# RWKV-5 attention and soft-MoE slots on one core: diagonal product from SBUF copies, one masked state product, a gated first weight, halved first output tiles

## The chip, the cores and the metric

The kernel runs on one core of a Trainium2 chip. A core has TensorE (PE, with its weight loads shown as PEld), VectorE (DVE), ScalarE (ACT), GpSimd (POOL) and SyncE (SP), which run their own instruction streams and meet through semaphores, and 16 DMA engines that serve the queues of SP and POOL. The metric is the device time of one execution in microseconds (us). The kernel before takes 125.46 us (median of three runs, 125.38 to 126.85).

## What is computed

The first stage is a linear attention with a decaying state, for batch 4, 8 heads, sequence 768, head size 48. The second is a soft mixture of experts over all 3072 rows of 384 values, with 8 experts, 4 slots each and a hidden size of 1024.

```python
for t in range(S):
    kt, vt, rt = (k[:, :, t], v[:, :, t], r[:, :, t])
    cur = np.einsum('bhd,bhe->bhde', u[None] * kt, vt)
    y[:, :, t] = np.einsum('bhd,bhde->bhe', rt, state + cur)
    state = w[None, :, :, None] * state + np.einsum('bhd,bhe->bhde', kt, vt)
...
x = y.transpose(0, 2, 1, 3).reshape(B * S, H * D)
logits = x @ phi
# d: softmax of logits over the rows, c: softmax over the slots
slot_input = d.T @ x
for e in range(E):
    h = np.maximum(slot_input[e] @ w1[e], 0.0)
    slot_out[e] = h @ w2[e]
out = c @ slot_out
```

The term with u is the diagonal: for each row, the sum over d of r, u and k at that row, times v.

## The kernel before

**Units.** Two heads side by side (96 columns, or 2 x 64 partitions after a transpose) make a unit m; there are 4 batches x 4 pairs of heads = 16 units. Each unit is cut into G = 2 halves of T = 384 rows, and each half into L = 3 chunks of 128 rows. The loop variable i counts halves: i = 2m for the first, 2m + 1 for the second, 32 in all, and it starts at -5 so that loads and transposes of later units run ahead.

**Steps of a half or a unit**, with the engine that does them:

- `scale` (L228, POOL; DVE for unit 0): k and r from `raw` times a table of powers of w (`W`), into `kr` in bf16. Three `kr` tiles rotate.
- `t_pe` (L235, PE): six transposes each of k (into PSUM bank T0, in even iterations) and r (into T1, in odd ones); `t_evac` (L241, ACT) copies them to `kT` and `rT` in SBUF.
- `b_pe`, `b_evac` (L247 PE, L252 DVE): k back to rows, `kn`.
- `prod_f` (L257, DVE): r times k, element by element, with r read from T1 and k from `kT`, both in a strided order. `prod` goes to PE (L329) to be summed against u.
- `a_pe`, `mask_f` (L299 PE, L304 DVE): the 128 x 128 blocks of r and k products for the chunks, masked into `AT`.
- `m_pe` (L314, L325, L329, PE): state products and diagonal sums in the PSUM bank Mb. `z_evac` (L339, L343, L345, DVE) takes them out: `Z0` (the state carried to the second half, times w to the power T, only for g = 0), `Z` (the states inside the half), both masked with `bmask` to the two heads' blocks, and `dv` (v times the diagonal sums).
- `y_pe`, `y_evac` (L355, L366, L368 PE, L375 ACT): the half's output.
- `v_cast`, `v_pe`, `v_evac` (L270, L284, L290): v to bf16, reordered through PE.

Every engine's stream is in the order in which the program is written; the helper `O` keeps it. In iteration i DVE gets `mask_f(i+1)`, in even iterations `prod_f`, then `z_evac(i+1)`, and in odd ones the copy to `kn`. PE gets `a_pe(i+1)`, `y_pe(i)`, `v_pe(i+2)`, `m_pe(i+1)`, routing steps (from i = 8 on, for the batch before: transposes of x, logits with phi, dispatch sums) and the transposes.

**Loads.** SP's queue holds the inputs: k, r and v of batches 0 and 1 in quarters, phi, then batches 2 and 3 as one transfer each of k, r and v. Three `raw` tiles hold the batches; batch 3 goes into that of batch 0. POOL's queue holds the weights, cast to bf16 on the way: eight of w1, eight of w2 (the last in three pieces), issued between the `kr` products as the table `W_AT` says. w2 goes into `raw` 1 and 2 when their batches are done.

**End.** The slot inputs `uns`, the expert matmuls (L594, then transposes L617, then L627), the division by the softmax sums over rows (`so`), row sums of the other softmax (L608, with their reciprocals L610), and 24 output tiles (L646 PE; L648 DVE and L650 ACT scale them), stored by SP and POOL in groups of 1, 1, 2, 4, 4, 4, 4, 4 tiles (L652).

Of the kernel before, what the change touches and what calls it, by code (L numbers as in the profile page):

```python
# [9 lines left out]
def kernel(  # L10
# [106 lines left out]

    def load_batch(b, step):
        for h0 in range(0, H, step):
            load_kr(0, k, b, h0, h0 + step)  # L120
            load_kr(1, r, b, h0, h0 + step)
            load_v(b, h0, h0 + step)

    load_batch(0, 2)
    load_batch(1, 2)
    O(sp.dma_start(out=phi_f[:], in_=moe_phi.rearrange("(mo p) s -> p mo s", p=128)))
    load_batch(2, H)
# [16 lines left out]
    O(pool.iota(s_i, pattern=[[-1, J]], base=T - 1, channel_multiplier=-J))  # L144
    ident_f = cst.tile([128, 128], f32, name="ident_f")
    O(pool.memset(ident_f[:], 0.0))
    O(pool.affine_select(out=ident_f[:], in_=ident_f[:], compare_op=ALU.not_equal, fill=1.0, base=0,
                         pattern=[[-1, 128]], channel_multiplier=1))
# [19 lines left out]
    ident = cst.tile([128, 128], bf, name="ident")  # L168
    O(dve.tensor_copy(ident[:], ident_f[:]))

# [25 lines left out]
    ex(1, 1)  # L196
    bmask = cst.tile([128, P2], f32, name="bmask")
    ones = cst.tile([128, 128], bf, name="ones")
    ucol = cst.tile([128, nQ, 2], bf, name="ucol")
    Le_t = [cst.tile([128, L, 128], bf, name=f"Le{j}") for j in range(2)]  # L200
    uns = cst.tile([128, nM, 2, EG, 32], bf, name="uns")
    O(pool.memset(bmask[:], 0.0))
    O(pool.memset(bmask[0:64, 0:D], 1.0))
    O(pool.memset(bmask[64:128, D:P2], 1.0))
    O(pool.memset(ones[:], 1.0))
    O(pool.memset(ucol[:], 0.0))
    for t in Le_t:
        O(pool.memset(t[:], 0.0))
    O(pool.memset(uns[:], 0.0))
    O(pe.transpose(Mb[:, 0:8], wu[:], ident_f[0:8, 0:8]))  # L210
# [43 lines left out]
    def prod_f(m):  # L254
        pr = wk.tile([128, S], bf, name="prod", bufs=2)
        st["prod", m] = pr
        O(dve.tensor_mul(pr[:].rearrange("p (s j) -> p s j", j=J),  # L257
                         T1[:, 0:S].rearrange("p (j s) -> p s j", j=J),
                         st["kT", m][:].rearrange("p (s j) -> p s j", j=J)))

# [71 lines left out]
    def z_evac(i):  # L332
        m, b, q, g, n = at(i)
        dv = wk.tile([128, L * 2, D], bf, name="dv", bufs=2)
        st["dv", i] = dv
        if g == 0:
            Z0 = wk.tile([128, P2], bf, name="Z0", bufs=2)
            st["Z0", m] = Z0
            O(dve.scalar_tensor_tensor(out=Z0[:], in0=Mb[:, 2 * P2:3 * P2], scalar=wT[:, q:q + 1],  # L339
                                       in1=bmask[:], op0=ALU.mult, op1=ALU.mult))  # L340
        Z = wk.tile([128, 2, P2], bf, name="Z", bufs=2)
        st["Z", i] = Z
        O(dve.tensor_mul(Z[:], Mb[:, 0:2 * P2].rearrange("p (c e) -> p c e", c=2),  # L343
                         bmask[:, None, :].to_broadcast([128, 2, P2])))
        O(dve.tensor_mul(dv[:], st["v", i][:].rearrange("p c e d -> p (c e) d"),  # L345
                         Mb[:, 288:288 + 2 * L, None].to_broadcast([128, L * 2, D])))

    def y_pe(i):
# [9 lines left out]
        for c in range(L):  # L358
            if c == 0:
                if g == 0:  # L360
                    continue
                z = st["Z0", m][:]
# [29 lines left out]
    def xt_ev(n, c, xt=None, eng=None):  # L392
        xT = wk.tile([128, Dm], bf, name="xT", bufs=4)
        st["xT", n, c] = xT
# [70 lines left out]

    W_AT = {13: 1, 14: 1, 15: 1, 16: 1, 18: 1, 19: 1, 21: 1, 22: 1, 23: 1, 25: 1, 26: 5}
    T_AT = {-4: [(dve, 0, 2), (dve, 1, 2), (act, 0, 2)], -3: [(act, 1, 2), (dve, 0, 3)],
            -2: [(act, 0, 3)], -1: [(dve, 1, 3), (act, 1, 3)]}
    nw = 0
    n0, n1 = nG - 2, nG - 1  # L470
    Wf = [t[:].rearrange("p q j d -> p (q j d)") for t in W]
    xs = Wf[0].bitcast(bf)[:, 2 * F:2 * F + 2 * L * Dm].rearrange("p (n m c t) -> p n m c t", n=2, m=nM, c=L)

# [141 lines left out]
    for g in range(2):  # L615
# [22 lines left out]
    obuf = ([raw[0][:, 16 * Dm:17 * Dm], raw[0][:, 17 * Dm:18 * Dm], Wf[0][:, 0:2 * Dm], Wf[1][:, 0:4 * Dm]]  # L638
            + [raw[0][:, x * 4 * Dm:(x + 1) * 4 * Dm] for x in range(4)])
    i = 0  # L640
    for gi, sz in enumerate(sizes):
        o_s = obuf[gi][:, 0:sz * Dm].rearrange("p (n m) -> p n m", m=Dm)
        i0 = i
        for j in range(sz):
            op = ob[i % 6][:, 0:Dm]
            O(pe.matmul(op, LexpT[:, i:Nn:nN], so[:], start=True, stop=True))  # L646
            if i % 2 == 0:
                O(dve.tensor_scalar_mul(o_s[:, j, :], op, rsr[:, i:i + 1]))  # L648
# [36 lines left out]
```

## Time and profile before

| what | value |
|---|---|
| median of three runs | 125.46 us |
| profiled execution, its own time | 124.32 us |
| its span in the trace | 122.5 us |
| mean granted TensorE clock | 0.967 |
| busy: PE, DVE, ACT, POOL | 100.0, 97.3, 84.2, 62.5 us |
| DVE products, prod L257 | 16 x 947 ns |
| DVE products, AT L304 | 32 x 950 ns |
| DVE, Z0 L339; Z L343; dv L345 | 16 x 317; 32 x 347; 32 x 444 ns |
| POOL, kr L228 | 30 x 1459 ns |
| HBM read, written | 39.38 MB, 4.72 MB |

An engine's busy time is the sum of its instructions. Two instructions that follow each other directly overlap by some tens of ns in these records, so the time that one takes in a row of its kind is its distance from start to start. The rows of forty digits cut the span into slices of 3.06 us. The chain of waits goes back from the last instruction: at each step to what released it, or to the instruction before it on its engine. A name in square brackets behind a row of the timeline is what ended the idle time before it.

### The profile page before, as it was taken

How to read it: one execution, taken by the hardware profiler on the slowest of the kernel's cores; microseconds unless marked ns; L12 is line 12 of the kernel's file. 1: busy time of each engine (PE TensorE's matmuls, PEld its weight loads, DVE VectorE, ACT ScalarE, POOL GpSimd, SP SyncE). 2: the span in 40 equal slices, each digit the busy share in tenths (PEclk: the TensorE clock that was granted, in tenths of full speed). 3: DMA queues.
4: the chain of work that ended last, by engine and by line, in shares of the span. 5: the costliest groups of instructions: out<-in, count | busy, mean ns of one | idle time of the engine just before them, and what ended most of it. 6: DMA issues, size and time to landing. Idle time of an engine off the chain costs nothing.

```text
span 122.5 us, 4329 instructions
## 1 busy us (share of the span) xinstructions
PE 100.0 (82%) x1784; PEld 80.5 (66%) x1785; DVE 97.3 (79%) x200; ACT 84.2 (69%) x176; POOL 62.5 (51%) x75
## 2 busy tenths in 40 slices
PE   5698988898898998989899898999979799994000
PEld 1356866686687877979778797777878549962000
DVE  1998899999999999899999999999978235598000
ACT  4479768777868798886889887788858253397000
POOL 5899999995756778494687758110000000011100
PEclk9999999999999999999999999999999999999655
DMA  2999999999999999999999999999999992069992
GB/s 66 290 372 374 372 372 366 347 388 362 328 384 372 324 217 215 212 219 212 217 218 211 220 209 215 216 217 218 215 214 215 210 193 49 5 235 395 401 415 94
DMA packets 21093, 31.79 MB, mean 259 GB/s; under 512 B 1361, under 2 KB 18258, under 8 KB 21074
## 3 DMA queue, kind: packets, MB, share of 16 engines
q0 software_dynamic: 3088, 14.95, 55.1%
q1 hardware_dynamic: 17986, 16.57, 40.1%
q8 instruction: 14, 0.23, 0.7%
q14 instruction: 5, 0.04, 0.1%
HBM read 39.38 MB, written 4.72 MB: 360 GB/s over the span
## 4 chain that ended last, share of the span: by engine, by line
DVE 38%; PE 31%; issue 11%; POOL 7%; ACT 4%; DVEq 1%; POOLq 1%; ACTq 0%
DVE prod L257 11%; DVE AT L304 8%; DVE dv L345 6%; DVE Z L343 5%; PE Vb L284 5%; DVE raw L648 3%; PE Mb L325 3%; PE Yb L368 3%; PE T L235 3%; PE T L425 2%; PE T L247 2%; POOL kr L228 2%; PE Ab L299 1%; DVE kn L252 1%; ACT W L484 1%
## 5 line engine op out<-in xcount | busy, mean ns | idle before, releaser
L228 POOL TENSOR_TENSOR kr<-raw,W 128x576 bf16<-128x576 f32 x30 | 43.2, 1459 | 14.6 <-PE T L235 11.1
L304 DVE TENSOR_TENSOR AT<-Ab,mask_ut 128x768 bf16<-128x768 f32 x32 | 30.4, 950 | 1.0 <-PE Ab L299 1.0
L284 PEld LDWEIGHTS <-Q 128*128 128x128 bf16 x288 | 16.2, 100 | 3.6 <-issue 2.9
L284 PE MATMUL Vb<-v_bf,Q 128*128 128x96 bf16 x288 | 18.2, 211 | 0.0
L235 PE MATMUL T<-ident,kr 128*128 128x128 bf16 x192 | 17.0, 230 | 0.2 <-POOL kr L228 0.2
L241 ACT COPY rT<-T 128x768 bf16<-128x768 bf16 x16 | 12.8, 798 | 6.0 <-PE T L235 2.7
L241 ACT COPY kT<-T 128x768 bf16<-128x768 bf16 x16 | 12.8, 799 | 5.1 <-PE T L235 4.8
L257 DVE TENSOR_TENSOR prod<-T,kT 128x768 bf16<-128x768 bf16 x16 | 15.1, 947 | 0.0
L375 ACT CAST x<-Yb 128x288 bf16<-128x288 f32 x32 | 13.1, 410 | 2.8 <-PE Yb L368 2.8
L652 POOL DMA_DIRECT2D out_dram<-W x1 | 0.5, 541 | 27.2 <-ACT raw L650 27.2
L345 DVE TENSOR_TENSOR dv<-vn,Mb 128x288 bf16<-128x288 bf16 x32 | 14.2, 444 | 0.0
L366 PE MATMUL Yb<-Z,rT 128*128 128x96 bf16 x80 | 10.5, 204 | 3.8 <-DVE Z L343 3.8
L290 ACT CAST vn<-Vb 128x288 bf16<-128x288 f32 x32 | 13.1, 409 | 0.5
L235 PEld LDWEIGHTS <-kr 128*128 128x128 bf16 x192 | 12.6, 102 | 1.1 <-DVE kr L228 0.5
L299 PE MATMUL Ab<-rT,kT 64*128 64x128 bf16 x192 | 11.1, 222 | 0.6 <-DVE AT L304 0.5
L325 PE MATMUL Mb<-vn,kn 128*128 128x96 bf16 (+2 forms) x80 | 11.5, 243 | 0.0
L343 DVE TENSOR_TENSOR Z<-Mb,bmask 128x192 bf16<-128x192 f32 x32 | 11.1, 347 | 0.0
L355 PE MATMUL Yb<-vn,AT 128*128 128x48 bf16 x192 | 10.3, 185 | 0.0
L368 PE MATMUL Yb<-dv,ident 128*128 128x288 bf16 x32 | 9.1, 284 | 1.4
L270 ACT CAST v_bf<-raw 128x576 bf16<-128x576 f32 x15 | 10.1, 676 | 0.0
L252 DVE COPY kn<-T 128x768 bf16<-128x768 bf16 x16 | 8.9, 555 | 1.4 <-PE T L247 0.7
L355 PEld LDWEIGHTS <-AT 128*128 128x128 bf16 x192 | 6.9, 96 | 3.2
(141 smaller groups left out, 209.4 us busy)
## 6 DMA issues: line engine op xcount, KB each, us to landing
w_all<-in_moe_w_dram POOLq DMA_DIRECT2D x8, 768.0 KB, 10.3
raw<-in_moe_w_dram POOLq DMA_DIRECT2D x7, 768.0 KB, 14.7
raw<-in_k_dram SPq DMA_DIRECT2D x8, 288.0 KB, 6.1
raw<-in_r_dram SPq DMA_DIRECT2D x8, 288.0 KB, 6.0
raw<-in_v_dram SPq DMA_DIRECT2D x8, 288.0 KB, 6.1
raw<-in_k_dram SPq DMA_DIRECT2D x2, 1152.0 KB, 10.9
raw<-in_r_dram SPq DMA_DIRECT2D x2, 1152.0 KB, 9.9
raw<-in_v_dram SPq DMA_DIRECT2D x2, 1152.0 KB, 13.1
```

What stands on the lines that cost most here:

```text
L228: O(eng.tensor_mul(kr[:, j].rearrange("p j (h s) -> p j h s", s=64)[:, :, :, 0:D], src, W[j][:, q].rearrange("p j (h d) -> p j h d", h=2)))
L235: O(pe.transpose(bank[:, x * C:(x + 1) * C], kr[:, j, x, :], ident[:]))
L241: O(act.copy(t[:].rearrange("p (s j) -> p s j", j=J), bank[:, 0:S].rearrange("p (j s) -> p s j", j=J)))
L257: O(dve.tensor_mul(pr[:].rearrange("p (s j) -> p s j", j=J), T1[:, 0:S].rearrange("p (j s) -> p s j", j=J), st["kT", m][:].rearrange("p (s ...
L284: O(pe.matmul(Vb[:, c * P2:(c + 1) * P2], Q3[:, o:o + C], vb[:, :, g, j, :], start=(j == 0), stop=(j == JV - 1)))
L290: O(act.copy(vn[:].rearrange("p c e d -> p (c e d)"), Vb[:, 0:L * P2]))
L304: O(dve.tensor_mul(AT[:], Ab[:, :, 0:T].rearrange("p e (c t) -> p e c t", c=L), mask_ut[:, None, None, :].to_broadcast([128, 2, L, C])))
L325: O(pe.matmul(o, kn[:, g * L + c, :], vc, start=first, stop=True, skip_group_check=True))
L343: O(dve.tensor_mul(Z[:], Mb[:, 0:2 * P2].rearrange("p (c e) -> p c e", c=2), bmask[:, None, :].to_broadcast([128, 2, P2])))
L345: O(dve.tensor_mul(dv[:], st["v", i][:].rearrange("p c e d -> p (c e) d"), Mb[:, 288:288 + 2 * L, None].to_broadcast([128, L * 2, D])))
L355: O(pe.matmul(Yb[:, o:o + D], AT[:, e, c, :], vn[:, c, e, :], start=first, stop=False, skip_group_check=True))
L375: O(act.copy(st["x", n][:, :, q * P2:(q + 1) * P2], Yb[:, 0:L * P2].rearrange("p (c e) -> p c e", c=L)))
```

## The change

- `prod_f` reads r from `rT` in SBUF instead of the PSUM bank T1, both operands in plain order, and stands behind `z_evac(i+1)` instead of ahead of `y_pe(i)`.
- `bmask` becomes a table `zt` per pair of heads, with three blocks of 96 columns, the third multiplied by w to the power T. One product gives Z and Z0 (288 columns for g = 0, 192 for g = 1). POOL fills the table at the start.
- The last batch's v is loaded as three quarters and one quarter. A one-column copy on POOL (`guard`) of the first piece stands ahead of the first weight, and `W_AT` moves the first weights from i = 13, 14 to 15 (two at once).
- `phi_f` and `ident_f` lie in `LexpT`, `uns` in a part of the table `W[1]` (zeroed at i = 28 instead of the start), and `xT` has two buffers instead of four.
- The first two output tiles are each computed and scaled in two halves of 192 columns, one on DVE, one on ACT. The reciprocals of the row sums are issued apart from the sums and later.

```diff
@@ loads
-    def load_batch(b, step):
+    def load_batch(b, step, cut=0):
         for h0 in range(0, H, step):
             load_kr(0, k, b, h0, h0 + step)
             load_kr(1, r, b, h0, h0 + step)
-            load_v(b, h0, h0 + step)
+            load_v(b, h0, h0 + step - cut)
+            if cut:
+                load_v(b, h0 + step - cut, h0 + step)
...
@@ start
-    bmask = cst.tile([128, P2], f32, name="bmask")
+    zt = cst.tile([128, nQ, 3, P2], f32, name="zt")
...
-    O(pool.memset(bmask[:], 0.0))
-    O(pool.memset(bmask[0:64, 0:D], 1.0))
-    O(pool.memset(bmask[64:128, D:P2], 1.0))
+    O(pool.memset(zt[:], 0.0))
+    O(pool.memset(zt[0:64, :, :, 0:D], 1.0))
+    O(pool.memset(zt[64:128, :, :, D:P2], 1.0))
...
-    O(pool.memset(uns[:], 0.0))
...
+    O(pool.tensor_mul(zt[:, :, 2, :], zt[:, :, 2, :], wT[:, :, None].to_broadcast([128, nQ, P2])))
...
@@ prod_f
-        O(dve.tensor_mul(pr[:].rearrange("p (s j) -> p s j", j=J),
-                         T1[:, 0:S].rearrange("p (j s) -> p s j", j=J),
-                         st["kT", m][:].rearrange("p (s j) -> p s j", j=J)))
+        O(dve.tensor_mul(pr[:], st["rT", m][:], st["kT", m][:]))
...
@@ z_evac
+        x = 3 if g == 0 else 2
+        Z = wk.tile([128, x, P2], bf, name=f"Z{g}", bufs=2)
+        st["Z", i] = Z
         if g == 0:
-            Z0 = wk.tile([128, P2], bf, name="Z0", bufs=2)
-            st["Z0", m] = Z0
-            O(dve.scalar_tensor_tensor(out=Z0[:], in0=Mb[:, 2 * P2:3 * P2], scalar=wT[:, q:q + 1],
-                                       in1=bmask[:], op0=ALU.mult, op1=ALU.mult))
-        Z = wk.tile([128, 2, P2], bf, name="Z", bufs=2)
-        st["Z", i] = Z
-        O(dve.tensor_mul(Z[:], Mb[:, 0:2 * P2].rearrange("p (c e) -> p c e", c=2),
-                         bmask[:, None, :].to_broadcast([128, 2, P2])))
+            st["Z0", m] = Z[:, 2, :]
+        O(dve.tensor_mul(Z[:], Mb[:, 0:x * P2].rearrange("p (c e) -> p c e", c=x), zt[:, q, 0:x, :]))
...
@@ loop
-    W_AT = {13: 1, 14: 1, 15: 1, 16: 1, 18: 1, 19: 1, 21: 1, 22: 1, 23: 1, 25: 1, 26: 5}
+    W_AT = {15: 2, 16: 1, 18: 1, 19: 1, 21: 1, 22: 1, 23: 1, 24: 1, 25: 1, 26: 5}
...
-        if odd == 0 and 0 <= mu + 1 < nU:
-            prod_f(mu + 1)
...
             z_evac(i + 1)
+        if odd == 0 and 0 <= mu + 1 < nU:
+            prod_f(mu + 1)
...
         if i == 3:
-            load_batch(3, H)
+            load_batch(B - 1, H, 2)
...
+        if i == min(W_AT):
+            O(pool.tensor_copy(guard[:], raw_of(2, B - 1)[:, 0:1]))
+        if i == 28:
+            O(pool.memset(uns, 0.0))
...
@@ output
+    def emit(i, bank, dst, x0, x1, eng):
+        op = ob[bank % 6][:, 0:x1 - x0]
+        O(pe.matmul(op, LexpT[:, i:Nn:nN], so[:, x0:x1], start=True, stop=True))
+        if eng is dve:
+            O(dve.tensor_scalar_mul(dst[:, x0:x1], op, rsr[:, i:i + 1]))
+        else:
+            O(act.activation(out=dst[:, x0:x1], in_=op, func=AF.Copy, scale=rsr[:, i:i + 1]))
...
+            if i < 2:
+                emit(i, 2 * i, o_s[:, j, :], 0, HD, dve)
+                emit(i, 2 * i + 1, o_s[:, j, :], HD, Dm, act)
             else:
+                emit(i, i + 2, o_s[:, j, :], 0, Dm, (dve, act)[i % 2])
             i += 1
+            if i == 2:
+                row_recip(8, 16)
+            if i == 6:
+                row_sums(16, nN)
+            if i == 8:
+                row_recip(16, nN)
```

More of the change, by code (lines that the diff above doesn't have):

```diff
@@ L98 @@
     warm = LexpT[:, 2048:2560]
+    late = LexpT[:, 2560:3072].bitcast(f32)
+    ident_f = late[:, 0:128]
+    phi_f = late[:, 128:128 + nM * ES].rearrange("p (m s) -> p m s", m=nM)
     wu = cst.tile([8, 128], f32, name="wu")
     wu3 = wu[:].rearrange("q (e s) -> q e s", s=64)
-    phi_f = cst.tile([128, nM, ES], f32, name="phi_f")
     O(act.preload_act_table_set("natural_log_exp_and_others"))
@@ L121, in load_batch @@
             load_kr(1, r, b, h0, h0 + step)
-            load_v(b, h0, h0 + step)
+            load_v(b, h0, h0 + step - cut)
+            if cut:
+                load_v(b, h0 + step - cut, h0 + step)
     load_batch(0, 2)
     load_batch(1, 2)
-    O(sp.dma_start(out=phi_f[:], in_=moe_phi.rearrange("(mo p) s -> p mo s", p=128)))
+    O(sp.dma_start(out=phi_f, in_=moe_phi.rearrange("(mo p) s -> p mo s", p=128)))
     load_batch(2, H)
@@ L144 @@
     O(pool.iota(s_i, pattern=[[-1, J]], base=T - 1, channel_multiplier=-J))
-    ident_f = cst.tile([128, 128], f32, name="ident_f")
-    O(pool.memset(ident_f[:], 0.0))
-    O(pool.affine_select(out=ident_f[:], in_=ident_f[:], compare_op=ALU.not_equal, fill=1.0, base=0,
+    O(pool.memset(ident_f, 0.0))
+    O(pool.affine_select(out=ident_f, in_=ident_f, compare_op=ALU.not_equal, fill=1.0, base=0,
                          pattern=[[-1, 128]], channel_multiplier=1))
@@ L168 @@
     ident = cst.tile([128, 128], bf, name="ident")
-    O(dve.tensor_copy(ident[:], ident_f[:]))
+    O(dve.tensor_copy(ident[:], ident_f))
     keep_warm(4)
@@ L200 @@
     Le_t = [cst.tile([128, L, 128], bf, name=f"Le{j}") for j in range(2)]
-    uns = cst.tile([128, nM, 2, EG, 32], bf, name="uns")
-    O(pool.memset(bmask[:], 0.0))
-    O(pool.memset(bmask[0:64, 0:D], 1.0))
-    O(pool.memset(bmask[64:128, D:P2], 1.0))
+    O(pool.memset(zt[:], 0.0))
+    O(pool.memset(zt[0:64, :, :, 0:D], 1.0))
+    O(pool.memset(zt[64:128, :, :, D:P2], 1.0))
     O(pool.memset(ones[:], 1.0))
@@ L217 @@
     O(act.activation(out=wT[:], in_=wT[:], func=AF.Exp, scale=float(T)))
+    O(pool.tensor_mul(zt[:, :, 2, :], zt[:, :, 2, :], wT[:, :, None].to_broadcast([128, nQ, P2])))
     phi_s = cst.tile([128, nM, ES], bf, name="phi_s")
     acc = cst.tile([128, NA], f32, name="acc")
+    guard = cst.tile([128, 1], f32, name="guard")
     st = {}
@@ L361, in y_pe @@
                     continue
-                z = st["Z0", m][:]
+                z = st["Z0", m]
             else:
@@ L392, in xt_ev @@
     def xt_ev(n, c, xt=None, eng=None):
-        xT = wk.tile([128, Dm], bf, name="xT", bufs=4)
+        xT = wk.tile([128, Dm], bf, name="xT", bufs=2)
         st["xT", n, c] = xT
@@ L471 @@
     Wf = [t[:].rearrange("p q j d -> p (q j d)") for t in W]
+    uns = Wf[1].bitcast(bf)[:, 2 * F:2 * F + nM * ES * 8].rearrange("p (m g j x) -> p m g j x", m=nM, g=2, j=EG)
     xs = Wf[0].bitcast(bf)[:, 2 * F:2 * F + 2 * L * Dm].rearrange("p (n m c t) -> p n m c t", n=2, m=nM, c=L)
@@ L609, in row_sums, with row_recip @@
                         start=(i == a), stop=(i == z - 1), skip_group_check=True))
+    def row_recip(a, z):
         O(dve.reciprocal(rsr[:, a:z], Mb[:, a:z]))
@@ L621 @@
             row_sums(0, 8)
+    row_recip(0, 8)
     SO = [Xb[:, 0:HD], Yb[:, 0:HD]]
@@ L644 @@
         for j in range(sz):
[L645 to L648, printed above, removed]
+            if i < 2:
+                emit(i, 2 * i, o_s[:, j, :], 0, HD, dve)
+                emit(i, 2 * i + 1, o_s[:, j, :], HD, Dm, act)
             else:
-                O(act.activation(out=o_s[:, j, :], in_=op, func=AF.Copy, scale=rsr[:, i:i + 1]))
+                emit(i, i + 2, o_s[:, j, :], 0, Dm, (dve, act)[i % 2])
             i += 1
+            if i == 2:
[4 more added lines that the diff above has]
+                row_recip(16, nN)
         O((sp, pool)[gi % 2 if gi > 1 else 0].dma_start(out=out_v[:, i0:i, :], in_=o_s))
-        if gi == 2:
-            row_sums(16, nN)
 _INS = ['r', 'k', 'v', 'w', 'u', 'moe_phi', 'moe_w1', 'moe_w2']
```

## The prediction

> **What bounds the kernel now.** I read the page's busy shares and its 40 slices first, to find which resource never rests.
>
> ```profile
> PE 100.0 (82%) x1784; PEld 80.5 (66%) x1785; DVE 97.3 (79%) x200; ACT 84.2 (69%) x176; POOL 62.5 (51%) x75
> ...
> DVE  1998899999999999899999999999978235598000
> ...
> DMA  2999999999999999999999999999999992069992
> GB/s 66 290 372 374 372 372 366 347 388 362 328 384 372 324 217 215 212 219 212 217 218 211 220 209 215 216 217 218 215 214 215 210 193 49 5 235 395 401 415 94
> ```
>
> DVE is at 9 tenths through the attention loop (to about 92 us), and so is the DMA row, from 3 us to 101 us. Two things therefore run side by side: DVE's loop, and one unbroken stream of transfers, first the inputs (about 370 GB/s), then the MoE weights (about 215 GB/s). Whichever is last decides when the expert matmuls can end. The table of stretches shows where the stream changes over, and the DMA answer for the last weight piece (issued at 81.49) when it lands.
>
> ```profile
> core 0: us, PE busy (x) PEld busy (x) DVE busy (x) ACT busy (x) POOL busy (x), PEclk, DMA share, GB/s
> 2.00:40.00 38.00, 32.91 (x473) 25.00 (x472) 34.97 (x70) 28.17 (x55) 32.74 (x38) 1.00 1.07 356
> 40.00:42.00 2.00, 2.00 (x44) 1.77 (x42) 1.94 (x5) 1.54 (x5) 1.50 (x3) 1.00 1.21 349
> 42.00:44.00 2.00, 1.73 (x34) 1.28 (x32) 2.00 (x5) 1.58 (x3) 1.64 (x2) 1.00 1.11 242
> 44.00:100.00 56.00, 51.14 (x1035) 43.22 (x1038) 48.57 (x101) 43.63 (x100) 24.21 (x28) 1.00 1.04 214
> 100.00:104.00 4.00, 4.00 (x116) 3.25 (x112) 2.10 (x5) 1.77 (x3) 0.00 (x0) 1.00 0.48 86
> ```
>
> ```profile
> L134 POOL DMA_DIRECT2D raw<-in_moe_w_dram x1: 527/527/527, 81.5 to 81.5; - x1
> ...
> DMA to landing us min/median/max: 22.3/22.3/22.3
> ```
>
> The DMA share is 1.0 or more in every stretch up to 100, so no time is free in the stream. The last w2 piece (steps y = 6 and 7 of expert 7) lands at 81.49 + 22.3 = 103.8. Its first reader, step y = 6 of the second half of L627, is due at 105.0 (in the chain the L627 matmuls run from 102.61 to 105.36, 0.17 for a step y of each half). The slack is only 1.2 us: **a faster loop alone gains at most that; a later stream costs all beyond it.**
>
> **The loop.** One pair of iterations costs DVE, start to start in the timeline from 31.56: AT 0.87, prod 0.86, Z 0.26, dv 0.36, AT 0.86, idle 0.28, Z0 0.23, Z 0.27, dv 0.36, kn 0.47: 4.8 us. PE waits about 0.7 to 0.9 in such a pair (for Z, dv, and Ab), and about 0.55 where routing is interleaved.
>
> *prod from SBUF.* 16 times. The trace has no bf16 product with both operands in SBUF. Upper end: today's row, 0.95 (the f32 products of L182, 744 ns for 576 elements, give the same at 768). Lower end: the 768-element bf16 copy to kn, 0.56. I take the lower one, as the price most favourable to the change, and keep 0.95 for the top of the range: a gain of 0.40 a pair, or none. For comparison only: the Trainium skill, "VectorE: DVE Perf Modes", section "The perf-mode tier table", gives a bf16 tensor_tensor in SBUF two elements a cycle, and its (N/2 + 150) cycles would make 0.56 of it, an estimate from that page; no run here shows it, and by it the sum stays as it is.
>
> *One Z product.* Z0 (0.23) goes, Z grows by 96 columns (0.10 at the 0.96 elements/ns of AT): gain 0.13. With dv no longer behind prod, PE's next steps start 0.86 earlier, and the idle 0.28 of DVE goes too. Together up to 0.8 a pair, and PE (about 4.0 us of work) would be next.
>
> *What comes back.* POOL's kr scaling reads two SBUF tiles. The loop products of DVE today each read PSUM, so they never meet it; the L182 products at the start do:
>
> ```profile
> 9.34 1.21 DVE L182 TENSOR_TENSOR W<-LexpT,sr 128x576 f32<-128x576 f32 x1
> 11.02 0.56 DVE L252 COPY kn<-T 128x768 bf16<-128x768 bf16 x1 [0.47 <-PE T L247]
> 11.50 0.94 DVE L182 TENSOR_TENSOR W<-LexpT,sk 128x576 f32<-128x576 f32 x1
> ```
>
> ```profile
> 8.87 1.06 POOL L268 CAST v_bf<-raw 128x576 bf16<-128x576 f32 x1
> 9.90 1.92 POOL L228 TENSOR_TENSOR kr<-raw,W 128x576 bf16<-128x576 f32 x1
> ```
>
> Alone they take 0.74. The first ends at 10.55, 0.62 after POOL's cast (9.93); the second at 12.44, 0.62 after POOL's kr (11.82). And that kr took 1.92 instead of 1.41, ending 1.27 after the DVE product. Each waited for the other to finish. So a prod that meets a kr waits for up to 1.36 (kr's start-to-start time). Where it falls in steady state:
>
> ```profile
> 62.85 0.95 DVE L257 TENSOR_TENSOR prod<-T,kT 128x768 bf16<-128x768 bf16 x1
> 62.89 0.50 PE L235 MATMUL T<-ident,kr 128*128 128x128 bf16 x6
> 63.55 1.40 POOL L228 TENSOR_TENSOR kr<-raw,W 128x576 bf16<-128x576 f32 x1 [0.38 <-PE T L235]
> ```
>
> In the new order Z and dv (0.62) stand in prod's place and prod's turn is at 63.47, 0.08 before kr: a coin toss. Without routing PE's transposes end sooner: prod's turn is 32.43 + 0.62 = 33.05, kr runs 32.64 to 34.04, so prod waits 1.0. Earlier still POOL runs thirteen kr back to back (9.90 to 29.25): mean wait 0.68. Per pair: -0.8 + 0.68 to 1.0, that is -0.1 to +0.2. Behind a waiting prod stand DVE's next AT and PE's diagonal matmuls (L329), and behind these the transposes that release POOL. Over the five pairs up to the first weight I count 0.1. The rule that speaks against the change is in the skill's "SBUF — State Buffer", section "Who interferes with whom": a DVE instruction with two SBUF inputs and a GpSimd one that reads SBUF exclude each other for the whole instruction, whoever starts first. Read merely as a slowing (0.20 and 0.47 in the two rows) the pairs would gain 0.4 each and the first weight come 2 us sooner; by the rule the sum stays.
>
> *Start.* POOL gets longer before its first kr, and that kr is on the chain:
>
> ```profile
> 9.90 1.93 POOL kr L228
> 11.83 0.05 issue
> 11.88 0.82 PE T L235 x6
> ```
>
> Its memsets run at (0.745 - 0.209)/640 = 0.84 ns an element. The table zt of 1152 columns costs 1.07, its two half fills of 576 cost 0.58 each, its product with wT (384 elements, between ucol's 0.60 for 4 and kr's 1.41 for 576) 1.14: 3.4. Gone: bmask 0.17 + 0.13 + 0.13, uns 0.74: 1.2. Less 0.1 for overlapping starts, +2.1 on the loop, bounds +1.2 (zt product at 0.60, half fills hidden) to +2.5. The uns memset returns at i = 28 behind the w2 issues, which queue far ahead of the stream: nothing. Smaller xT rings, ident_f and phi_f moved: nothing, each buffer's reader is one iteration on.
>
> **The first weight.** Before, it is issued at 39.48, behind POOL's seventeenth kr, while the inputs still flow. After, the guard copy and the first two weights stand behind the nineteenth kr, and wait for three quarters of the last v. That kr starts at 42.91 now; with +2.1, +0.1, and PE's transposes standing 0.6 earlier in their iteration, at 44.5. It ends at 45.9; the guard is 0.1: issue at 46.0. From issue to flow: the first weight, issued at 39.48, shows in the 41 to 42 us stretch (346 GB/s, then 259), so 2.0: flow from 48.0. The inputs alone end at 42.7 (40.0 plus the 0.95 MB left at about 350 GB/s). The stream stands empty for 5.3 us. Of this 0.8 returns, since the first weight no longer shares the engines with v's tail (it took 8.4 us to land, where 768 KB at 214 GB/s take 3.7, plus 2.0 of start and 1 to 2 of the input bytes). The last piece lands at 103.8 + 5.3 - 0.8 = 108.3, 3.3 past need. The loop (+2.1 + 0.1, seven routed pairs at +0.1, three last ones without kr at -0.5: +1.4 at its end) is covered by this. The POOL queue behind the guard holds the kr of later pairs, which are two pairs ahead of their readers: nothing.
>
> **Output tail.** The first tile's halves take 0.42 (the so row, 128x192) instead of 0.61 on one engine, and the reciprocal moves behind them: the first store leaves 0.2 to 0.5 earlier. The stores then run at 400 GB/s, so this is a shift of the end: -0.3. The other tiles and the moved row sums are covered by the stores.
>
> **Sum:** 5.3 - 0.8 - 1.2 - 0.3 = +3.0 us. The profiled execution is 124.32 (span 122.5 and 1.8 around it), the median of the three runs 125.46: 127.3 for a profiled run, **128.5** for the median. About 2% (2.5 us) is what a measurement of this kernel can tell from no change.
>
> **Rivals.**
> 1. *The guard waits for v alone.* If prod wins its coin tosses, pairs shrink by 0.5 to 0.8 and the nineteenth kr is done when v lands, about 43.2. Issue 43.4, flow 45.4, empty 2.7: 2.7 - 0.8 - 1.2 - 0.3 = +0.4, 125.9. For it: PE's idle time per pair. Against: the start's +2.1 and the 1.0 wait without routing.
> 2. *Not slower: the stream evens out.* From 100 to 104 it moves 86 GB/s: the engines end apart. At 214 these 344 KB would take 1.6 us, so an even end gains 2.2. With case 1's start the landing is 103.8 + 2.7 - 2.2 = 104.3, and the loop, 2 us faster by then, lets L627 end at 104.7 instead of 105.36: -0.7 - 0.3 = -1.0, 124.5. It decides only if the unevenness stems from the v tail. Against: the rate before 100 is no better for it.
> 3. *prod at 0.95 and waiting.* +0.4 a pair more, five pairs: first weight 2.0 later, +5.0, 130.5. For it: every two-input row of DVE here runs at one element a cycle.
>
> Chances: forecast 0.47, case 1 0.25, case 2 0.13, case 3 0.15. Faster by over 2% would need case 2 and a further 1.5 us, 0.05. The forecast's own spread is 127.3 to 129.7, some of it within 2%. Together: slower 0.52, same 0.43. The range runs from case 1 with a little of case 2 (125.2) to case 3 (130.4).
>
> **What would show it.** Right: a hole in the GB/s slices between 43 and 48 us; last w2 piece landing near 108; L627 on PE waiting for DMA; prod at 0.6 where no kr runs and 1 to 2 us where one does; the first POOL kr near 12. Wrong: no hole, first weight issued before 44, or L627 not waiting. Then the loop sets the end and cases 1 and 2 are judged by the pair time.

## The result, and the profile after

The changed kernel takes **131.94 us** (median of 4 runs, 131.53 to 132.35) against 125.42 for the kernel before, a ratio of **1.050**, 95% interval 1.041 to 1.059. It is slower, as forecast, but by 6.5 us instead of 3.0. Its profiled execution has a span of 130.0 us (131.82 with what lies around it), against 122.5 (124.32) before: 7.5 us more. That profiled run of before lay 1.1 us under its median, which is why the spans differ by more than the medians. Some executions of some kernels here are more than 1.5% longer than the fastest of the same kernel: the ratios, here and below, leave them out and no profile of such a one is used, but the medians keep them.

Three rows of the 40 slices, each slice now 3.25 us:

```profile
PEclk9999999999999999999999999999999996589755
...
DMA  2999999999999107999999999999999997057992
GB/s 73 313 368 376 374 366 313 339 388 351 351 384 348 55 0 132 213 212 215 212 217 219 217 217 217 212 213 214 215 216 219 214 202 144 9 218 296 408 408 121
```

The stream of transfers that was unbroken before has a hole where the inputs end and the weights begin, and the granted clock of PE, 9 tenths or more until the stores before, now falls in the 34th to 36th slice. The table of stretches shows both places closer:

```profile
core 0: us, PE busy (x) PEld busy (x) DVE busy (x) ACT busy (x) POOL busy (x), PEclk, DMA share, GB/s
...
42.00:44.00 2.00, 1.39 (x28) 1.10 (x24) 2.00 (x4) 1.50 (x5) 0.42 (x1) 1.00 0.37 115
44.00:46.00 2.00, 2.00 (x46) 1.77 (x46) 2.00 (x6) 1.62 (x4) 1.42 (x1) 1.00 0.05 12
46.00:48.00 2.00, 1.45 (x29) 1.11 (x28) 2.00 (x4) 1.92 (x4) 1.81 (x3) 1.00 0.00 0
48.00:50.00 2.00, 1.93 (x41) 1.71 (x42) 2.00 (x6) 1.50 (x5) 1.98 (x4) 1.00 0.27 25
...
105.00:107.00 2.00, 0.55 (x27) 0.32 (x16) 0.00 (x0) 0.00 (x0) 0.00 (x0) 1.00 1.03 204
107.00:109.00 2.00, 0.24 (x1) 0.09 (x1) 0.00 (x0) 0.00 (x0) 0.00 (x0) 0.75 1.06 196
109.00:111.00 2.00, 0.98 (x28) 0.98 (x31) 0.00 (x0) 0.00 (x0) 0.00 (x0) 0.50 0.39 68
```

From 44 to 48 us the DMA engines move next to nothing. From 105.5 to 110 DVE, ACT and POOL stand still, and PE too but for 0.24 us, while the weights still flow, and PE comes out of that at half its clock. What it waits for is in PE's timeline:

```profile
107.00 0.24 PE L633 MATMUL Xb<-raw,W 128*32 128x192 bf16 x1 [1.45 <-DMA raw<-in_moe_w_dram]
110.02 0.32 PE L633 MATMUL Xb<-raw,W 128*32 128x192 bf16 x1 [2.78 <-DMA raw<-in_moe_w_dram]
```

and the last weight piece, issued at 89.71, answers when the stream ends:

```profile
L138 POOL DMA_DIRECT2D raw<-in_moe_w_dram x1: 530/530/530, 89.7 to 89.7; - x1
DMA to landing us min/median/max: 22.1/22.1/22.1
```

It lands at 111.8; before it landed at 103.8. So the stream is 8.0 us late at its end, and it is late because it started late. POOL's timeline at that place:

```profile
44.24 1.42 POOL L231 TENSOR_TENSOR kr<-raw,W 128x576 bf16<-128x576 f32 x1 [1.82 <-PE T L250]
46.19 1.41 POOL L231 TENSOR_TENSOR kr<-raw,W 128x576 bf16<-128x576 f32 x1 [0.53 <-PE T L238]
47.54 0.52 POOL L543 COPY guard<-raw 128x1 f32<-128x1 f32 x1
48.00 1.18 POOL L135 DMA_DIRECT2D w_all<-in_moe_w_dram  x2
```

The guard copy comes right behind the nineteenth kr, with no idle time of its own. The three quarters of v that it asks for had landed at 43.6 (issued at 33.07, 10.5 to landing), so what held the first weight for 4 us was POOL's own queue. And the nineteenth kr starts at 46.19 instead of 42.91, as this line of before has it:

```profile
42.91 1.40 POOL L228 TENSOR_TENSOR kr<-raw,W 128x576 bf16<-128x576 f32 x1 [0.36 <-PE T L235]
```

Of these 3.3 us 1.4 are there from POOL's first kr on, which starts at 11.33 instead of 9.90. The rest stands in DVE's timeline between 29 and 41 us:

```profile
29.25 0.94 DVE L260 TENSOR_TENSOR prod<-rT,kT 128x768 bf16<-128x768 bf16 x1
30.12 2.77 DVE L540 CAST phi_s<-LexpT 128x32 bf16<-128x32 f32 x3
...
36.36 1.41 DVE L260 TENSOR_TENSOR prod<-rT,kT 128x768 bf16<-128x768 bf16 x1
...
41.25 1.59 DVE L260 TENSOR_TENSOR prod<-rT,kT 128x768 bf16<-128x768 bf16 x1
```

The first nine prods, up to 57 us, take between 0.94 and 1.76, the last seven, which find no kr under way, 0.54 to 0.55 (in three of these pairs it is kr that waits, 1.62 to 1.75 instead of 1.40). The line that the prediction did not look at is the second one: three casts of 32 elements take 2.77. Before, they took 0.48:

```profile
28.97 0.48 DVE L541 CAST phi_s<-phi_f 128x32 bf16<-128x32 f32 x3
```

Meanwhile POOL ran kr without a pause:

```profile
23.95 8.90 POOL L231 TENSOR_TENSOR kr<-raw,W 128x576 bf16<-128x576 f32 x6
```

These six end at 32.85, and the AT product behind the casts starts at 32.81. Taken one by one, two of the casts take 1.38 us each and one 0.17; the last kr of the six starts at 31.43, between the two long ones.

### The profile page after: what moved, and what is told of

It is laid out like the page before. It is cut to its first block, busy times and chain, and to the rows that moved or that the text cites. A ratio compares the mean times of both kernels' runs of the same rounds, so it can differ in the third digit from the quotient of the medians.

```text
span 130.0 us, 4301 instructions
## 1 busy us (share of the span) xinstructions
PE 101.5 (78%) x1786; PEld 81.6 (63%) x1787; DVE 98.8 (76%) x185; ACT 83.2 (64%) x177; POOL 66.8 (51%) x77
## 4 chain that ended last, share of the span: by engine, by line
DVE 31%; DMA 22%; PE 18%; POOL 8%; issue 8%; ACT 6%; POOLq 1%; DVEq 0%; ACTq 0%
DMA raw<-in_moe_w_dram 22%; DVE prod L260 8%; DVE AT L305 8%; DVE dv L343 4%; DVE Z L342 4%; PE T L238 3%; DVE kn L255 3%; DVE raw L650 2%; PE T L250 2%; PE Ab L300 2%; PE Vb L285 2%; PE Xb L388 1%; ACT v_bf L271 1%; ACT kT L244 1%; ACT rT L244 1%
## 5 line engine op out<-in xcount | busy, mean ns | idle before, releaser
L231 POOL TENSOR_TENSOR kr<-raw,W 128x576 bf16<-128x576 f32 x30 | 44.9, 1516 | 14.3 <-PE T L238 10.4
L285 PE MATMUL Vb<-v_bf,Q 128*128 128x96 bf16 x288 | 18.1, 211 | 0.1
L285 PEld LDWEIGHTS <-Q 128*128 128x128 bf16 x288 | 16.2, 100 | 1.8 <-issue 0.5
L260 DVE TENSOR_TENSOR prod<-rT,kT 128x768 bf16<-128x768 bf16 x16 | 17.0, 1066 | 0.0
L342 DVE TENSOR_TENSOR Z<-Mb,zt 128x288 bf16<-128x288 f32 (+1 forms) x32 | 12.7, 396 | 0.6 <-PE Mb L330 0.5
L300 PEld LDWEIGHTS <-kT 64*128 64x128 bf16 x192 | 5.7, 95 | 7.6 <-issue 2.8
L138 POOL DMA_DIRECT2D raw<-in_moe_w_dram x10 | 5.5, 552 | 8.9 <-DMA raw<-in_moe_w_dram 6.8
L330 PE MATMUL Mb<-ucol,prod 128*128 128x2 bf16 x96 | 7.1, 166 | 3.0 <-DVE prod L260 2.8
## 6 DMA issues: line engine op xcount, KB each, us to landing
raw<-in_k_dram SPq DMA_DIRECT2D x2, 1152.0 KB, 10.5
```

Source lines behind the costliest of these rows:

```text
L231: O(eng.tensor_mul(kr[:, j].rearrange("p j (h s) -> p j h s", s=64)[:, :, :, 0:D], src, W[j][:, q].rearrange("p j (h d) -> p j h d", h=2)))
L260: O(dve.tensor_mul(pr[:], st["rT", m][:], st["kT", m][:]))
L285: O(pe.matmul(Vb[:, c * P2:(c + 1) * P2], Q3[:, o:o + C], vb[:, :, g, j, :], start=(j == 0), stop=(j == JV - 1)))
L300: O(pe.matmul(Ab[:, e, c * C:(c + 1) * C], kT[s, t], rT[s, t]))
L342: O(dve.tensor_mul(Z[:], Mb[:, 0:x * P2].rearrange("p (c e) -> p c e", c=x), zt[:, q, 0:x, :]))
```

## The experiments

Two theories stood against each other at the start. **A, the stream:** the gate (guard, later table of issues) puts the first weight behind a POOL queue that the held-up DVE instructions make late, and the end of the weight stream sets the end of the kernel. **B, the loop:** the attention loop is slower by itself, and the hole in the stream would have been hidden.

The table gathers what the profiles of all kernels show, one row to a run. "First weight" is its issue on POOL; "last landing" the issue of the last w2 piece and its time to landing; a dash stands where there is no profile to use. The ratios and the medians need not agree in the last digits. Each kernel has one profile, so its first four columns of times are those of one execution.

| kernel | first weight | last landing | first store | span | median | ratio to before (95%) |
|---|---|---|---|---|---|---|
| before | 39.48 | 103.8 | 106.93 | 122.5 | 125.4 | 1 |
| after | 48.00 | 111.8 | 114.25 | 130.0 | 131.94 | 1.050 (1.041 to 1.059) |
| a1, no gate | 41.76 | 105.0 | 107.56 | 123.5 | 125.88 | 1.006 (1.001 to 1.012) |
| a2, gate alone | 44.37 | 108.1 | 110.23 | 126.1 | 129.28 | 1.023 (1.014 to 1.033) |
| a3, casts on ACT | 45.31 | 109.0 | 111.28 | 126.7 | 128.49 | 1.022 (1.014 to 1.029) |
| a4, PE kept busy | 47.38 | 110.9 | 112.78 | 128.2 | 130.08 | 1.036 (1.027 to 1.045) |
| b1, prod from PSUM | 46.74 | 110.7 | 112.81 | 129.0 | 130.35 | 1.040 (1.033 to 1.048) |
| b2, zt on DVE | 50.22 | 113.9 | 116.06 | 131.5 | 133.29 | 1.068 (1.060 to 1.076) |
| d2, casts on ACT and prod from PSUM | 44.58 | 108.7 | 110.62 | 126.0 | 127.18 | 1.019 (1.012 to 1.026) |
| d1, as d2, no gate | 38.20 | 104.0 | 106.28 | 121.9 | 124.44 | 0.996 (0.991 to 1.001) |
| d3, casts on ACT, no gate | 39.68 | 104.0 | 105.91 | 121.3 | **123.18** | **0.988 (0.982 to 0.993)** |
| c1, as d1, old place of prod, zt on DVE | 41.26 | 104.1 | 108.84 | 124.7 | 125.09 | 1.000 (0.996 to 1.004) |
| c2, as d3, zt on DVE | - | - | - | - | 125.16 | 0.990 (0.982 to 0.998) |
| d4, as d1, zt bf16 on DVE | 39.17 | 103.2 | 107.25 | 123.1 | 125.54 | 0.997 (0.992 to 1.002) |

**The law in it.** Take the first two columns. For every kernel whose first weight leaves at 41.26 or later, the last landing minus that issue is 62.8 to 64.1 us (c1 and d2 are the ends). For those that issue it at 39.7 or earlier the landing stays at 103.2 to 104.0, however early the issue. So there is a knee near 40 to 41 us: up to there an earlier issue buys nothing, beyond it each microsecond of delay is a microsecond at the end of the stream.

The gate has two parts, and no run takes them apart, but the timelines do. In each of the seven kernels with a guard the copy starts directly behind the nineteenth kr, with no idle time before it, so it never waited for v. What it asks for cost nothing; the later place of the first weight in the table, two kr further down POOL's queue, and the copy itself (0.46 us up to the issue in after, a3 and a4, 0.12 or 0.13 in the others) are what the gate costs.

### a1_no_gate

```
-    W_AT = {15: 2, 16: 1, 18: 1, 19: 1, 21: 1, 22: 1, 23: 1, 24: 1, 25: 1, 26: 5}
+    W_AT = {13: 1, 14: 1, 15: 1, 16: 1, 18: 1, 19: 1, 21: 1, 22: 1, 23: 1, 25: 1, 26: 5}
...
-            load_batch(B - 1, H, 2)
+            load_batch(3, H)
...
-        if i == min(W_AT):
-            O(pool.tensor_copy(guard[:], raw_of(2, B - 1)[:, 0:1]))
```

> The changed kernel without the gate: no guard copy, the old table of weight issues (first weight at iteration 13), v of the last batch in one transfer. Theory A (the hole in the transfer stream sets the end): the first weight now stands behind POOL's seventeenth kr, 41.0 to 42.4 in the trace of after, instead of the nineteenth and the guard (48.0). Issue near 42.5, flow near 44.4, so the hole shrinks from 7 us to about 2; the last w2 piece lands 4 to 5 us earlier (107 instead of 111.8) and PE no longer idles long enough to lose its clock: about 127, between 126 and 128. Theory B (the loop, 1.4 us later at its end and held up by prod's exclusion with kr, sets the end; the hole would have been hidden): stays at 131 to 132.

Measured: first weight at 41.76, last landing 105.0, 125.88 us, 6.1 below after. L631 (the expert product) no longer waits for DMA. Theory A. Nearly the whole loss hangs on the gate; what is left, 0.5 us, goes with the loop, later than before at its end by 0.8 (the scaling of so starts at 106.2 instead of 105.4). Part of that need not be the program's: the granted clock of PE was 0.50 from 22 to 24 us in this execution, where after and before have 1.00, and the third prod starts at 25.70 instead of 24.82 in after.

### a2_gate_alone

```
-    def load_batch(b, step):
+    def load_batch(b, step, cut=0):
...
-            load_v(b, h0, h0 + step)
+            load_v(b, h0, h0 + step - cut)
+            if cut:
+                load_v(b, h0 + step - cut, h0 + step)
...
+    guard = cst.tile([128, 1], f32, name="guard")
...
-    W_AT = {13: 1, 14: 1, 15: 1, 16: 1, 18: 1, 19: 1, 21: 1, 22: 1, 23: 1, 25: 1, 26: 5}
+    W_AT = {15: 2, 16: 1, 18: 1, 19: 1, 21: 1, 22: 1, 23: 1, 24: 1, 25: 1, 26: 5}
...
-            load_batch(3, H)
+            load_batch(B - 1, H, 2)
...
+        if i == min(W_AT):
+            O(pool.tensor_copy(guard[:], raw_of(2, B - 1)[:, 0:1]))
```

> The kernel before with the gate alone: guard copy, the new table of weight issues, v of the last batch split; the products, the tables and the output tiles as before. Theory A (a later stream costs all beyond the slack of 1.2 us): the nineteenth kr ends at 44.3, as in the trace of before, issue near 44.6, flow near 46.5, a hole of 3.6 to 3.9 us; last landing 107.4 to 107.7, end +2.4 to +3.2, so 128 to 129. If POOL's kr is not the last of the waits, v is (about 43), issue 43.2: +1.5, 127. Theory B (the gate costs nothing, the loop's changes do): 125.4.

Measured: first weight at 44.37, behind a nineteenth kr at 42.90, last landing 108.1, 129.28 us, ratio 1.023 (1.014 to 1.033). Theory A, a little over what it expected (landing 107.4 to 107.7, 128 to 129 us). So the gate costs 2.3% with the old loop, the rest of the change 0.6%, and both together 5.0%: more than their sum, which fits the table: behind the gate a delay of POOL's queue is a delay of the stream.

### a3_phi_act

```
-                O(dve.tensor_copy(phi_s[:, mi, :].rearrange("p (j g s) -> p g j s", g=2, s=Spe),
+                O(act.copy(phi_s[:, mi, :].rearrange("p (j g s) -> p g j s", g=2, s=Spe),
```

> The changed kernel with the three casts phi_f to phi_s on ACT instead of DVE. They took 2.77 us on DVE in after, where POOL's kr ran back to back (0.48 before). Theory A (casts from SBUF to SBUF and kr exclude each other on DVE; this delay passes through AT, PE and POOL to the nineteenth kr and the first weight): casts about 0.9 to 1.5 us on ACT without a stall, first weight 1.5 to 2.3 us earlier than 48.0, end earlier by as much: 129.5 to 130.5. Theory B (the delay is absorbed before the nineteenth kr, since POOL and PE catch up): first weight still at 47.5 to 48, 131 to 132.

Measured: 128.49, which is 3.4 less than after, more than expected. ACT's timeline has the three casts at 0.46 in all, although POOL runs the same six kr beside them:

```profile
30.01 0.46 ACT L540 CAST phi_s<-LexpT 128x32 bf16<-128x32 f32 x3
```

The nineteenth kr starts at 43.50 instead of 46.19 and the first weight leaves at 45.31, 2.7 earlier; the last landing follows, 2.8 earlier; the rest, 0.5, lies behind the landing, where the clock of PE is back at 1.00 by 111 us here and not before 115 in after. So three tiny casts, which nobody would count, delayed this kernel by 2.7 us at the first weight; the four times of a3 (128.44 to 128.92) and of after (131.53 to 132.35) lie well apart.

### a4_clock

```
+                    if g == 1 and y == 0 and x == 0:
+                        busy({2: 7, 3: 14}.get(j, 0))
```

> The changed kernel with 7 and 14 extra matmuls (their results unused) in the last expert product, put where PE stands waiting for the last three weight pieces, so that it does not idle for 1.7 and 3 us. Theory A (the idle time lowers the granted PE clock to 0.5, and the lower clock costs 0.6 us in the last matmuls after the landing and some more in the row sums and the first output product): PEclk stays at 1.0 from 105 to 113, four matmuls take 0.08 instead of 0.16, end 0.6 to 1.0 us earlier: 131.0 to 131.3. Theory B (the clock is lowered by something else, or the last matmuls are hidden): clock 0.5 as before or no change of time.

`busy(n)` issues n matmuls whose results nothing reads.

Measured: 130.08, better than expected. The table of stretches of this kernel:

```profile
105.00:107.00 2.00, 2.00 (x10) 0.79 (x9) 0.00 (x0) 0.00 (x0) 0.00 (x0) 1.00 1.05 206
107.00:109.00 2.00, 2.00 (x11) 0.88 (x9) 0.00 (x0) 0.00 (x0) 0.00 (x0) 1.00 0.93 166
109.00:111.00 2.00, 2.00 (x57) 1.30 (x59) 0.00 (x0) 0.00 (x0) 0.00 (x0) 1.00 0.15 26
```

The clock stays at 1.00 with PE kept busy, while the weights arrive almost as late as in after: Theory A. Four matmuls of the last product follow each other in 0.08 instead of 0.16. The gain of 1.9 is not all of the clock at the end: the first weight left 0.6 earlier and the last piece landed 0.9 earlier, because the phase of DVE against POOL fell otherwise. In this execution the granted clock was 0.50 from 22 to 25 us (1.00 in after): nine matmuls of L285 took 0.93 instead of 0.54, DVE waited 0.87 for PE, and the third prod started at 25.80 instead of 24.82. From there two prods took 1.32 and 1.41 instead of 0.95 and 0.94, and the casts met no kr:

```profile
31.93 0.34 DVE L540 CAST phi_s<-LexpT 128x32 bf16<-128x32 f32 x3
```

So which instruction waits, and how much, is partly chance; the nineteenth kr started at 45.57, still 2.1 later than in a3. Counted from the last landing to the end of the span, 130.0 - 111.8 = 18.2 for after and 128.2 - 110.9 = 17.3 here: by this one pair of profiles the half clock at the end costs **0.9 us**.

### b1_prod_psum

```
-        O(dve.tensor_mul(pr[:], st["rT", m][:], st["kT", m][:]))
+        O(dve.tensor_mul(pr[:].rearrange("p (s j) -> p s j", j=J),
+                         T1[:, 0:S].rearrange("p (j s) -> p s j", j=J),
+                         st["kT", m][:].rearrange("p (s j) -> p s j", j=J)))
```

> The changed kernel with its gate, but prod reads r from PSUM again (the strided view of T1), at its new place behind Z and dv. Theory A (prod with both operands in SBUF is held up by POOL's kr, and this is what makes the gate late): every prod takes 0.95 and none 1.4 to 1.8; the prods before the nineteenth kr lost 0.81, 0.69, 0.46 and 0.64 over 0.95 in after, together 2.6, so the first weight leaves near 45.4 instead of 48.0 and the end comes as much earlier: about 129.3, less the part that the phi_s casts may still lose. Theory B (the later start of POOL by 1.4 us and the order of the work set the nineteenth kr, the exclusion is hidden): first weight at 47.5 or later, 131 to 132.

Measured: 130.35, first weight at 46.74. Between the theories: prod is held up no more, but the casts still are.

```profile
28.38 0.95 DVE L260 TENSOR_TENSOR prod<-T,kT 128x768 bf16<-128x768 bf16 x1
29.25 2.59 DVE L542 CAST phi_s<-LexpT 128x32 bf16<-128x32 f32 x3
```

Every prod takes 0.94 or 0.95, and the three before the casts follow each other by 4.4 us, so with PSUM as its source prod and kr do not exclude each other. Of the 2.6 that I expected 1.3 came, since POOL's block of kr lasts to 31.7 and whichever instruction with SBUF sources DVE puts beside it waits. At the nineteenth kr the four kernels with a gate and the new POOL start compare like this: 46.19 with both on DVE and in SBUF (after), 43.50 without the casts (a3), 45.26 without prod (b1), 43.11 without either (d2, where nine matmuls of L287 took 0.93 near 18 us instead of 0.55 in d1, and the second prod starts 1.4 later than there; d1, without a gate, has 41.77). The casts are the larger share.

### b2_zt_dve

```
     O(dve.memset(one_f, 1.0))
+    zt = cst.tile([128, nQ, 3, P2], f32, name="zt")
+    O(dve.memset(zt[:], 0.0))
+    O(dve.memset(zt[0:64, :, :, 0:D], 1.0))
+    O(dve.memset(zt[64:128, :, :, D:P2], 1.0))
...
-    zt = cst.tile([128, nQ, 3, P2], f32, name="zt")
...
-    O(pool.memset(zt[:], 0.0))
-    O(pool.memset(zt[0:64, :, :, 0:D], 1.0))
-    O(pool.memset(zt[64:128, :, :, D:P2], 1.0))
...
-    O(pool.tensor_mul(zt[:, :, 2, :], zt[:, :, 2, :], wT[:, :, None].to_broadcast([128, nQ, P2])))
...
     def b_evac(m):
+        if m == 0:
+            O(dve.tensor_mul(zt[:, :, 2, :], zt[:, :, 2, :], wT[:, :, None].to_broadcast([128, nQ, P2])))
```

> The changed kernel with the table zt filled and multiplied on DVE instead of POOL, so that POOL's first kr starts near 9.3 instead of 11.33. Theory A (the longer start of POOL goes through to the gate one to one): first weight 1.4 to 2 us earlier than 48.0, end 130.0 to 130.5. Theory B (POOL runs its first kr back to back until 30 us and the loop is limited by DVE and its waits for kr there, so the start is absorbed): first weight within 0.5 of where it is, 131.5 to 132.

Measured: 133.29, worse than after. Neither theory, because the edit did not do what I meant: the fills on DVE took to 4.0, 1 us longer than DVE had been idle there, so W and wuT came 1.2 later, POOL waited for wuT, and its first kr started at 11.14, hardly earlier than 11.33.

```profile
8.80 0.57 POOL L214 TENSOR_TENSOR ucol<-wuT 64x4 bf16<-64x4 f32 x1 [2.91 <-DVE wuT L213]
...
11.71 1.76 DVE L253 TENSOR_TENSOR zt<-zt,wT 128x384 f32<-128x384 f32 x1
```

The multiplication by wT, moved from POOL to DVE, then waited for kr itself (1.76 for 384 elements). The first weight left 2.2 later than in after and the last landing came 2.1 later, so the run still serves the law of the table. What POOL's longer start alone costs stays open.

### c1_psum_no_gate and c2_sbuf_no_gate

c1 is a1 with prod from PSUM at its old place, the casts on ACT, zt filled on DVE as in b2 and multiplied on ACT; c2 is the same with prod from SBUF at the changed place.

> What the two traces point to: no gate (old weight issues, v uncut), prod from PSUM at its old place, phi_s casts on ACT, zt filled on DVE and multiplied on ACT, and from the change the one Z product and the halved first output tiles. Theory A (without lock and gate the transfer stream is unbroken until 103.8 and the loop ends before it, so the slack of 1.2 us comes free and the first store leaves 0.2 earlier): 124.0 to 124.6 against 125.35. Theory B (the one Z product and the ACT casts buy nothing that reaches the end): 125.3 to 125.8.

> As the kernel with prod from PSUM and no gate, but prod reads both copies from SBUF at the changed kernel's place. Theory A (prod's exclusion with kr costs the loop 0.1 to 0.2 a pair while kr runs, and 0.4 a pair is won back where it does not): the first weight, behind the seventeenth kr, leaves 1 us or more later than in that kernel; end 0.3 to 1.0 later, 124.6 to 125.5. Theory B (prod in SBUF pays once zt, casts and gate are out of the way): equal to it or faster.

Measured: 125.09 and 125.16 us, ratios 1.000 (0.996 to 1.004) and 0.990 (0.982 to 0.998). For c1 theory B: the last piece landed at 104.1, but the loop ended later than in before (so scaled from 107.4). In its profile POOL started at 11.14 as in b2, the pairs of the old order stayed at 4.73, and the granted clock of PE was 0.50 from 21 to 24 us; this execution, 126.48, was 1.4 us over the median, so the three are not weighed against each other. For c2 theory B too, against me: prod from SBUF was not the worse of the two, though c1 and c2 differ in prod's place as well.

### d1_psum_phi_no_gate, d2_psum_phi_gate, d3_sbuf_phi_no_gate

a1's edit (d1 and d3), a3's edit (all three) and b1's edit (d1 and d2) put together.

> No gate, the phi_s casts on ACT, prod from PSUM at its new place behind Z and dv; zt stays on POOL, the rest as the changed kernel. Theory A (the new order is worth 0.3 to 0.5 a pair once nothing in it can be held up by kr: in the gated kernel with prod from PSUM the prods followed each other by 4.4 us before the casts came, against 4.7 to 4.8 with the old order): first weight near 39 to 40, loop at the last expert product 1 us or more before the last landing (103.8), end 124.0 to 124.6. Theory B (POOL's kr and the start set the pace, not DVE): first weight at 41 or later and no better than 125.3.

> The changed kernel with its gate, with both remedies: prod from PSUM at the new place and the phi_s casts on ACT. Theory A (the two held-up groups of instructions make the gate late, and the last landing follows the first issue with 0.6 to 1.0 us less): nothing on DVE waits for kr, nineteenth kr at 42.5 to 43.3, first weight 44.0 to 44.8, last landing near 107.8, end 127.6 to 128.4. So about half of the loss of 6.5 us stays with the gate itself, as for the gate alone (129.3). Theory B (once DVE is not held up the gate costs nothing): 125.5 to 126.

> No gate, prod from SBUF at its new place, the phi_s casts on ACT, zt on POOL. Theory A (the casts are one of the two held-up groups; taking them off DVE brings the loop 2 us forward as it did with the gate): first weight near 39.6, end 124.3 to 125.0, between the kernel without the gate (125.9) and the same with prod from PSUM. Theory B (without a gate the stream sets the end anyway): 125.3 to 125.9.

Measured: 124.44, 127.18 and 123.18. d2 is Theory A, a shade better than expected: with neither prod nor the casts in kr's way, the first weight leaves at 44.58, the last piece lands at 108.7, and the kernel with the gate is still 1.9% (1.2 to 2.6) over before and 2.2% over d1, which is the same without the gate. d1 has the earliest first weight of all, 38.20, and lands its last piece at 104.0, as d3 does with 39.68: below the knee an earlier issue buys nothing. d3 beats both kernels of this case, by 1.2% (0.7 to 1.8) the one before. Its stream has no hole:

```profile
GB/s 43 312 360 374 373 367 368 289 384 373 324 382 379 356 236 214 216 213 218 213 215 214 217 216 211 218 217 208 221 216 211 221 198 140 9 258 386 393 421 97
```

It is faster than I expected (124.3 to 125.0), and I had put it behind d1. Its so scaling starts at 104.5 and d1's at 104.9. Of the prods in SBUF the first nine take up to 0.8 longer than 0.95 each, and the last seven, which find none under way, are 0.4 cheaper. The intervals of the two (0.982 to 0.993 and 0.991 to 1.001) overlap by little, and all four times of d3 (122.79 to 123.47) lie below all twelve of d1 (123.51 to 128.71). That SBUF is the better source without the gate is likely; by how much stays open.

### d4_zt_bf16

d1 with zt in bf16 (the factors of the state table rounded to it), filled on DVE and multiplied on ACT.

> As the kernel without gate, with casts on ACT and prod from PSUM, but zt is bf16 (its values rounded), filled on DVE in the 1.65 us in which DVE waits for s_i, and multiplied on ACT; POOL then has neither zt nor bmask nor uns before its first kr. Theory A (the start counts through the whole loop): first kr 9.3 or earlier instead of 11.3, loop 1 to 2 us earlier; the end gains only what is left of the slack, 0 to 0.5 us on that kernel. Theory B (the fills take longer than the wait, push sk, W and wuT back as the f32 fills on DVE did, 1.2 us): no gain or 0.5 us worse.

Measured: ratio 0.997 (0.992 to 1.002), the same as d1. POOL's first kr starts at 10.44 instead of 11.34, but the first prod at 14.26 instead of 13.29: the start moved from POOL to DVE. The span is 1.2 longer than d1's. Theory B.

## Why the prediction was wrong, point by point

The direction and most of the mechanism were right: a hole in the stream, weights late, L633 (L627 before) waiting for DMA, prod excluded by kr (0.94 to 1.76, and 0.543 where it did not wait, near the 0.56 that was taken), the first kr later (11.33; "near 12"). The size was wrong in four terms. Span for span the forecast was +3.0 and the result +7.5:

1. **"Issue at 46.0" was 48.0: 2.0 us.** The step that failed is "Over the five pairs up to the first weight I count 0.1". There the exclusion was priced for prod alone, and "Smaller xT rings, ident_f and phi_f moved: nothing, each buffer's reader is one iteration on" asked when the buffer of the casts is read, not what its reader meets on the way. The casts to phi_s read SBUF and write SBUF too. In before they met only the last 0.3 us of POOL's block of kr (0.48); with POOL 1.4 later they met its last two kr, and two of the three casts waited (2.77). The nineteenth kr, forecast for 44.5, starts at 46.19, 1.7 later. From 42.91 before, the forecast has +2.1 for POOL's start and 0.1 - 0.6 = -0.5 for what follows; measured are +1.43 and +1.85. With the casts on ACT (a3) the second is -0.84 and the nineteenth kr starts at 43.50: without the casts the pairs gain about as forecast, and the sum is even too high, because the start cost 1.4 and not 2.1. The last 0.3 to 0.4 us of the 2.0 is the guard, 0.46 to the issue instead of 0.1, beside a prod.
2. **"Of this 0.8 returns" was -0.6 to -0.7: 1.4 us.** By the table a first weight at 46.0 lands its last piece 62.8 to 64.1 later, near 109.7, not at 108.3. The gate-alone kernel shows it: empty from 42.7 to about 46.4, 3.7 us, landing +4.3. The prediction read it as a loss that in before the first weight shares the engines with v's tail; no run shows any of that coming back.
3. **The clock was not in the sum: 0.6 us** to the end of L633 (0.94 after the last landing instead of 0.36), 0.9 to the end of the span by a4.
4. **"The output tail: -0.3" did not show: 0.4 us.** From the scaling of so on ACT to the end of the span it is 17.1 before and 17.2 after. At full clock the new tiles gave 16.7 (d3), 16.9 (d1) and 17.3 (a1), so whether they gain anything is not settled; the half clock hides it here.

2.0 + 1.4 + 0.6 + 0.4 = 4.4, and 3.0 + 4.4 = 7.4 of the 7.5 measured.

Of the rivals, the first ("the guard waits for v alone") did not occur: v was there at 43.6 and POOL came at 47.54. The third (prod at 0.95 and waiting, first weight 2.0 later, +5.0) had the size and the place of the delay, but another cause: prod was 0.55 where it did not wait, and the casts and the guard brought the 2 us. The loop did end 1.4 later, hidden, as the forecast said (the last copy of LexpT on DVE at 98.78 instead of 97.37), but with luck: at the nineteenth kr it was 3.3 behind, where the forecast has 1.6, and it won 1.9 back by its end. Chance is also in the size of point 1: in a4, with the same program up to there, the casts met no kr.

The Trainium skill, "SBUF — State Buffer", section "Who interferes with whom", lists copies and casts, which can use both ports, beside two-input products among what contends with GpSimd for the shared port pair, and says that whoever issues first blocks the other for the whole instruction. The runs fit: 2.77 and 2.59 for casts beside kr, 0.34 where they met none (a4), 0.46 for the same casts on ACT. The prediction had applied the half of it that the diff pointed at.

## What to carry to other kernels

When a change delays an engine, list every instruction that will then meet it under a shared lock, the small and unchanged ones too: three casts worth 0.34 us cost 2.7 here. A transfer stream that is never idle should be given its next transfer before the last one ends, with as little computation ahead of it in its queue as can be; find the knee (here an issue at about 40 to 41 us, with inputs that end near 42.7), because up to it an earlier issue is worth nothing and past it each microsecond comes back whole at the end. And where the matrix engine will wait for such a stream, count the time that it may then run at a lower clock (0.9 us here).

## What the runs showed of the hardware that was not expected

- The granted clock of PE fell to 0.50 with waits of 1.45 and 2.78 us in after. The length of a wait does not settle it. In the gate-alone kernel, with waits of 1.09 and 1.80 us, the clock fell only about 1.7 us after PE had resumed: 1.00 from 108 to 109 with PE fully busy, 0.74 from 109 to 110, 0.50 from 110 to 112. In d2, with waits of 0.29 and 2.04 us before 109, it stayed at 1.00 up to 117.
- The clock also fell without any wait for DMA: 0.50 from 22 to 24 us in a1 and from 22 to 25 in a4, where after and a3, with the same work up to there, kept 1.00. It moved the third prod by 0.9 to 1.0 us and with it what met what.
- A series of short instructions fares worse beside a long one on the other side of the lock than one long instruction: 2.77 us for three casts (0.34 without kr), against at most 1.76 for a prod in the same run. Between two casts a kr that was waiting got its turn.
- The guard copy of one element a partition took 0.52 beside a prod with SBUF sources that ended at 48.01, and 0.19 to 0.20 in the three kernels with a guard whose prod reads PSUM.
